# A third seven-product block in chunk 0's feed-forward: four plain tiles regrouped, and the channel sums of w_out's first pieces moved ahead

## The chip, the cores and the metric

The kernel runs on one core of a Trainium2 chip. The metric is the device time of one execution in microseconds, as the median of several runs. A core has five engines with queues of their own: TensorE (PE in the profile; its weight loads are shown apart as PEld), VectorE (DVE), ScalarE (ACT), GpSimd (POOL) and SyncE (SP, which here only issues DMAs). Each engine works through its own queue in order; engines wait for each other through semaphores.

## What is computed

The reference is polysketch attention followed by an MLP with exact GELU:

```python
# q, k, v: (4, 4, 1088, 32) float32;  S1, S2: (8, 32)
def phi(x):
    a = np.einsum('rd,bhsd->bhsr', S1, x)
    b = np.einsum('rd,bhsd->bhsr', S2, x)
    return np.einsum('bhsi,bhsj->bhsij', a, b).reshape(*x.shape[:-1], 64)
q_p, k_p = phi(q), phi(k)
kv  = np.einsum('bhsf,bhsd->bhfd', k_p, v)
z   = np.sum(k_p, axis=2)
num = np.einsum('bhsf,bhfd->bhsd', q_p, kv)
den = np.einsum('bhsf,bhf->bhs', q_p, z)[..., None] + 1e-06
x   = (num / den).transpose(0, 2, 1, 3).reshape(4352, 128)
h   = x @ w_in                                  # w_in:  (128, 2048)
out = (0.5 * h * (1 + erf(h / sqrt(2)))) @ w_out  # w_out: (2048, 128)
```

The weights and the sketch matrices arrive as 64-bit floats; the kernel rounds them to 32 bits itself.

## The kernel before

**Tiling.** Tokens are worked on in nine chunks: eight of 512 tokens (two per batch entry, chunk 0 to 7) and a last one (chunk 8) with the 64 tokens that are left of each batch entry. d_ff is cut into 16 tiles of 128, numbered fi = 0 to 15. For each chunk n and tile fi, `hidden` (L740) multiplies a tile of w_in with the chunk's xT into a PSUM bank `h_ps` (two banks in rotation), and ACT applies GELU from there into SBUF (L747). The output of a chunk is accumulated in PSUM banks `o_ps` (two in rotation).

**Two ways to multiply with w_out.** A *plain* tile is one 128x512 matmul (`project`, L925) from a buffer `g` (four in rotation) into one bank. A *block* takes four tiles together. Each pair of tiles is a 2x2 problem, two halves of the tokens and two halves of the output channels, and is done with seven products of half size instead of eight (`two_products`, L826). The products are 64 output rows wide and 256 columns long; two run side by side on the two halves of TensorE, so a block is seven pairs. They need *token sums* (four combinations of GELU outputs, made on POOL in `token_sums`, L791 to L794, in buffers called bits_low, bits_a, bits_e, bits_m, in this order) and *channel sums* (four combinations of w_out, T1 to T4 in the buffers called small, made on POOL in `channel_sums`, L778 to L781, once for each of five pieces of w_out). The products are numbered: "4" and "7" use the first token sum (7) and T4 and T3, "6" uses bits_e, "1" and "5" use bits_a, "2" and "3" use bits_m. A block that opens a chunk's banks has the order 4/7 (two pairs), 6 (one), 1/5 (two), 2/3 (two). At the end of a chunk `drain` and `combine` put the products together, and the plain tiles' sum, copied out of its bank earlier by `take_usual` (L854, ACT), is added.

Before the change, chunks 0 and 1 have eight plain tiles each (`USUAL = 8`), then two blocks; chunks 2 to 7 have four blocks; chunk 8 has six pairs of another form.

**Pieces of the weights.** w_in and w_out are loaded in five pieces, columns 0 to 256, 256 to 512, 512 to 1024, 1024 to 1536, 1536 to 2048 (piece 0 to 4). Each is rounded by a chain of instructions in class `Rounding`: the low words scaled (`low_words`, L270, ACT), the exponent and mantissa fields (`fields`, L283 and L288, DVE), the exponents (`exponents`, L294, ACT), the mantissas (`mantissas`, L302, DVE), the signs (`signs`, L307, DVE) and the product (L312, DVE, or POOL for the last pieces). The token sums of the blocks use the same rotating buffers as this rounding, and the GELU outputs of a block use the big buffers in which the raw weights of pieces 2 to 4 landed.

**Order.** The order of each engine's queue is the order of the text; nothing is scheduled. `steps` lists (chunk, tile) one after the other: step t does `hidden` for its tile, then (if the tile ends a block) the token sums, then what has been hung on `slots[t]` with `at(t, ...)`, then `products[t]`. Before, the steps were chunk 0 tiles 0 to 3, chunk 1 tiles 0 to 3, chunk 0 tiles 4 to 7, chunk 1 tiles 4 to 7 (steps 0 to 15), chunk 0 tiles 8 to 15, chunk 1 tiles 8 to 15 (steps 16 to 31), then chunks 2 to 8. A plain product stands two steps after its tile (`LAG`). From step 18 on a hidden tile is two 64-row halves side by side. Slots used by the change and its neighbourhood: rounding of pieces 2 and 3 of both weights (slots 4 to 11), of w_in's piece 4 (12 and 13) and of w_out's piece 4 (14 and 15); `spread_sketches` on POOL (11); `widen_v_rem`, the v remainder, on POOL (12); the key transposes `key_turn_blocks` on DVE (14, L383); `features_of_all`, which multiplies the transposed keys with the sketches on PE (16, L1043); `outer_of_all` and `add_tokens` on DVE (16, 17), whose result `z_sum` and `kv_sum` on PE want at step 24 (L456).

Of the kernel before, what the change touches and what calls it, by code (L numbers as in the profile page):

```python
# [10 lines left out]
AX = mybir.AluOpType  # L11
# [5 lines left out]
def kernel(  # L17
# [18 lines left out]
    pe, dve, act, pool, sp = nc.tensor, nc.vector, nc.scalar, nc.gpsimd, nc.sync  # L36
# [5 lines left out]
    NF = d_ff // 128  # L42
# [7 lines left out]
    NCH = J // JC  # L50
    C = D + 1
    LAG = 2
    NMAIN = B * NCH
    NB = 4

    USUAL = 8
    BLOCKED = 12
    NCHUNK = NMAIN + 1
    assert B == 4 and d_model == 128 == H * D == JC * D == 2 * F and H == 4 and REM == 64 and NCH == 2
# [18 lines left out]
    def hidden_bank():  # L78
        return hps.tile([128, CW], FP, name="h_ps")

    def out_bank():
        return ops.tile([128, CW], FP, name="o_ps")


    by_act, by_dve, by_pool = act.copy, dve.tensor_copy, pool.tensor_copy
# [11 lines left out]
    w_in_sb = [big.tile([d_model, c1 - c0], FP, name=f"w_in{i}") for i, (c0, c1) in enumerate(pieces)]  # L97
    w_out_sb = [big.tile([128, c1 - c0], FP, name=f"w_out{i}") for i, (c0, c1) in enumerate(pieces)]
# [42 lines left out]
    def block(dtype=U32):  # L141

        b = big.tile([128, NB, 512], U32, name="block", bufs=3)
        return b if dtype == U32 else b.bitcast(dtype)
# [108 lines left out]
    class Rounding:  # L253
# [11 lines left out]
                self.low = self.lows[:rows, n:2 * n] if beside else self.lows[:rows, :n]  # L265
                self.m = mlp.tile([128, LC], FP, name="bits_m")[:rows, :n]

        def low_words(self):
            if self.wide:
                act.activation(out=self.low, in_=self.lo, func=ACT.Copy, scale=2.0 ** -52)  # L270

        def fields(self, by_dve=False):
# [454 lines left out]
    def w_tile(w, fi):  # L727
        i = max(i for i, (c0, c1) in enumerate(pieces) if c0 <= fi * 128)
        at = fi * 128 - CUTS[i]
        return w[i][:, at:at + 128]  # L730
# [3 lines left out]
    def hidden(n, fi, by_halves=False):  # L734
        W = width[n]
        ps = first_banks.pop((n, fi)) if (n, fi) in first_banks else hidden_bank()
        w = w_tile(w_in_sb, fi)
        for rows in (slice(0, 64), slice(64, 128)) if by_halves else (slice(0, 128),):
            if (n, fi) not in begun:
                pe.matmul(ps[rows, :W], lhsT=w[:, rows], rhs=xT[n][:, :W], start=True, stop=True)  # L740
        if n < NCH and fi < USUAL:
            g_of[n, fi] = mlp.tile([128, CW], FP, name="g", bufs=4)
        else:
            if fi % NB == 0:
                blocks[n, fi // NB] = block(FP)
            g_of[n, fi] = blocks[n, fi // NB][:, fi % NB]
        act.activation(out=g_of[n, fi][:, :W], in_=ps[:, :W], func=ACT.Gelu)  # L747
# [60 lines left out]
        return sums[n, b][j][:, e], T[j][:, k]  # L808

    def first_block(n):  # L810
        return USUAL // NB if n < NCH else 0

    def two_products(n, b, i):

        fours, ones_, sixes = [("4", "7", e, e) for e in range(2)], [("1", "5", e, e) for e in range(2)], ("6a", "6b", 0, 1)

        opens = b == first_block(n)
        order = fours + ([sixes] + ones_ if opens else ones_ + [sixes]) + [("2", "3", e, e) for e in range(2)]
        two = order[i]
        if opens and i == 0:  # L820
            acc[n] = [out_bank(), out_bank()]
        for name, e in zip(two[:2], two[2:]):
            half, bank, col = PLACE[name]
            moving, fixed = factor(n, b, name, e)

            pe.matmul(acc[n][bank][half * 64:(half + 1) * 64, col:col + HW], lhsT=fixed, rhs=moving,  # L826
                      start=opens and e == 0 and name in "4715", stop=b == NF // NB - 1, skip_group_check=True)
# [24 lines left out]
    def take_usual(n):  # L852
        usual[n] = mlp.tile([128, CW], FP, name="g", bufs=4)
        act.copy(out=usual[n], in_=o_of[n])  # L854
# [14 lines left out]
    def sums_rem(k):  # L869
        g = [g_of[NMAIN, 2 * k + i][:, :256].rearrange("p (half x) -> p half x", half=2) for i in range(2)]  # L870
        (a11, a21), (a12, a22) = ([a[:, h] for h in range(2)] for a in g)
        s = mlp.tile([128, CW], FP, name="g", bufs=4).rearrange("p (j x) -> p j x", j=4)
        eng = dve if k > 3 else pool
        eng.tensor_sub(out=s[:, 2], in0=a11, in1=a21)
        eng.tensor_add(out=s[:, 0], in0=a21, in1=a22)
        eng.tensor_sub(out=s[:, 1], in0=s[:, 0], in1=a11)
        eng.tensor_sub(out=s[:, 3], in0=a12, in1=s[:, 1])
        sums[NMAIN, k] = s
# [33 lines left out]
        drained[NMAIN] = to  # L912

    def project(n, fi, parts=range(B // 2), cols=slice(None)):
        first, final = fi == (BLOCKED if n == NMAIN else 0), fi == (USUAL if n < NCH else NF) - 1
        if first and n not in o_of:
            o_of[n] = out_bank() if n < NMAIN else [out_bank() for i in range(B // 2)]
        g = g_of[n, fi]
        if n == NMAIN:

            for i in parts:
                pe.matmul(o_of[n][i][:, :128], lhsT=g[:, i * 128:(i + 1) * 128], rhs=w_tile(w_out_sb, fi),  # L922
                          start=first, stop=final)
            return
        pe.matmul(o_of[n][:, cols], lhsT=w_tile(w_out_sb, fi), rhs=g[:, cols], start=first, stop=final)  # L925
# [35 lines left out]
    r = Rounding(SR)  # L961
# [64 lines left out]
        first_hidden(0, half)  # L1026


    steps = [(n, fi) for f in range(0, USUAL, 4) for n in range(NCH) for fi in range(f, f + 4)]
    steps += [(n, fi) for n in range(NCHUNK) for fi in range(USUAL if n < NCH else 0, NF)]  # L1030
    slots = {t: [] for t in range(len(steps) + LAG)}

    def at(t, f, *a):
        slots[t].append(lambda: f(*a))
# [85 lines left out]
            attend(n, banks)  # L1120
        take_kv(b, banks[:, 1, CW // 2:])

    def round_at(t, w, product_by=dve):
        r = []
        at(t, lambda: (r.append(Rounding(w)), r[0].low_words(), r[0].fields()))
        at(t + 1, lambda: (r[0].exponents(), r[0].mantissas(), r[0].signs(), r[0].product(product_by)))

    for i, (t0, t1) in enumerate(((4, 6), (8, 10))):
        round_at(t0, w_in_sb[i + 2])
        round_at(t1, w_out_sb[i + 2])  # L1130
    round_at(12, w_in_sb[4], pool)
    at(13, channel_sums, 3)

    at(12, widen_v_rem, 1)
    for r in range(2):
        at(14, key_turn_blocks, 1, r)
    round_at(14, w_out_sb[4], pool)
    at(15, query_turn, 2)
    at(16, features_of_all, 1)
    at(16, outer_of_all, 1)  # L1140
# [9 lines left out]
    at(24, query_sketch, 2)  # L1150
    at(26, lambda: turn_kv(1, held["kv"]))
    at(24, query_outer, 2)
    for i, t in enumerate((25, 26, 28)):
        at(t, channel_sums, i)
    at(11, spread_sketches)
    at(40, repeat_first_z)
    for n in range(3, NCHUNK):

        t = (n - 1) * NF
# [39 lines left out]
    products = {t: [] for t in range(len(steps) + LAG)}  # L1199
    done = {t: [] for t in range(len(steps) + LAG + 1)}  # L1200
    drains = {t: [] for t in range(len(steps) + LAG + 1)}
    for t, (n, fi) in enumerate(steps):
        if n < NCH and fi < USUAL:
            products[t + LAG].append((project, n, fi))
            if fi == USUAL - 1:
                slots[t + LAG + 1 + 2 * n].append(lambda n=n: take_usual(n))
        elif n == NMAIN:
            if fi % 2 and fi < BLOCKED:
                slots[t].append(lambda k=fi // 2: sums_rem(k))
            at_ = t + LAG  # L1210
            if fi == NF - 1:

                names = [(k, name) for k in range(BLOCKED // 2) for name in ORDER_REM]
                steps_rem = NF - 5
                for i, (k, name) in enumerate(names):
                    products[n * NF + 5 + i * steps_rem // len(names)].append((product_rem, k, name))
                products[n * NF + 4 + steps_rem].append((combine_rem,))

                products[at_] += [(project, n, NF - f, (i,)) for f, i in ((4, 0), (3, 0), (2, 0), (4, 1), (1, 0), (3, 1),
                                                                          (2, 1), (1, 1))]  # L1220
                done[at_ + 1].append(n)
        elif fi % NB == NB - 1:
            b = fi // NB
            opens = b == first_block(n)
            late = int(n < NCH or n == NCH and opens)
            for later, pairs in ((3, 3), (4, 2), (5, 2)) if opens else ((2, 2), (3, 2), (4, 1), (5, 2)):
                later += late
                for i in range(pairs):
                    products[t + later].append((two_products, n, b, len([p for q in products.values() for p in q
                                                                        if p[:3] == (two_products, n, b)])))  # L1230
            if b == NF // NB - 1:
                drains[t + 6 + late].append(n)
                done[t + (12 if n < NMAIN - 1 else 9)].append(n)

    for t in range(len(steps) + LAG):
# [40 lines left out]
        if t < len(steps):  # L1276
            n, fi = steps[t]
            hidden(n, fi, by_halves=t >= 18)
        if t < len(steps) and steps[t][0] < NMAIN and steps[t][1] % NB == NB - 1:
            n, b = steps[t][0], steps[t][1] // NB  # L1280
            if b >= first_block(n):
                token_sums(n, b)
# [48 lines left out]
```

## Time and profile before

| what | us |
|---|---|
| median of 3 runs (lowest, highest) | 258.04 (258.0, 258.37) |
| the profiled execution's own time | 257.91 |
| its span, first to last instruction | 256.1 |
| PE busy | 251.9 |
| POOL busy | 171.7 |
| DVE busy | 156.0 |
| ACT busy | 114.5 |
| hidden tiles (L740) on PE | 137.1 |
| plain products (L925) on PE | 16.5 |

The granted TensorE clock was 1.000 over the span. The page's table by engine counts the time in which an engine has an instruction under way; for PE the ends of matmuls are modelled, so the distance between the starts of two rows says more than a row's length. In a timeline row the columns are the start, the length, the engine, the line, the operation, output <- inputs with shape, and the number of instructions merged; behind it in brackets stands how long the engine was idle before and what ended that. A float32 matmul shows as two records.

### The profile page before, as it was taken

The page shows a single profiled execution, that of the slowest core. Times are in us where ns is not written, and L with a number is a line of the kernel's source. Part 1 is how long each engine was busy: PE and PEld are TensorE (multiplying, and loading weights), DVE is VectorE, ACT ScalarE, POOL GpSimd, SP SyncE. Part 2 cuts the span into 40 slices and gives each one's busy share as a digit, 9 for nine tenths or more (in the row PEclk, how much of TensorE's full clock was granted, in tenths as well). Part 3 has the DMA queues.
Part 4 walks back from the last instruction along what each step waited for, and adds up shares of the span by engine and source line. Part 5 has one row for each costly group of instructions (what it writes and reads, how often), then busy time and mean ns, then how long its engine had stood idle before and what let it go on. Part 6 is the DMA issues. An engine that isn't in the chain of part 4 may idle for free.

```text
span 256.1 us, 5952 instructions
## 1 busy us (share of the span) xinstructions
PE 251.9 (98%) x2407; PEld 131.5 (51%) x2407; DVE 156.0 (61%) x330; ACT 114.5 (45%) x221; POOL 171.7 (67%) x191
## 2 busy tenths in 40 slices
PE   8999999999999999999999999999999999999994
PEld 4755444255454545454444455455544444445784
DVE  4896889969698987580278976399307000700382
ACT  3784766523535333533335332623444334433541
POOL 3413008799969777587758774787758777877950
PEclk9999999999999999999999999999999999999999
DMA  6789548610001101101000001000200200020021
GB/s 209 217 280 292 153 122 205 204 26 12 0 3 17 25 4 23 21 13 31 0 3 0 0 15 31 1 4 0 38 6 7 37 0 4 5 36 3 0 36 31
DMA packets 29083, 13.50 MB, mean 53 GB/s; under 512 B 21888, under 2 KB 27264, under 8 KB 29056
## 3 DMA queue, kind: packets, MB, share of 16 engines
q1 hardware_dynamic: 28624, 12.79, 20.1%
q8 instruction: 19, 0.31, 0.5%
q10 hardware_dynamic: 432, 0.33, 0.4%
q14 instruction: 8, 0.07, 0.1%
HBM read 10.88 MB, written 2.23 MB: 51 GB/s over the span
## 4 chain that ended last, share of the span: by engine, by line
PE 98%; ACT 0%; DVE 0%; issue 0%
PE h_ps L740 45%; PE o_ps L826 33%; PE o_ps L925 5%; PE w_ps L896 2%; PE w_ps L456 1%; PE w_ps L604 1%; PE w_ps L659 1%; PE w_ps L957 1%; PE w_ps L570 1%; PE o_ps L922 1%; PE h_ps L756 1%; PE o_ps L445 1%; PE w_ps L1043 1%; PE h_ps L348 1%; PE w_ps L685 0%; PE o_ps L397 0%
## 5 line engine op out<-in xcount | busy, mean ns | idle before, releaser
L740 PE MATMUL h_ps<-xT,w_in 128*64 128x512 f32 (+2 forms) x536 | 137.1, 568 | 0.0
L747 ACT ACTIVATE block<-h_ps 128x512 f32<-128x512 f32 (+1 forms) x128 | 73.0, 571 | 116.3 <-PE h_ps L740 114.4
L826 PE MATMUL o_ps<-block,w_out 128*64 128x256 f32 x224 | 57.5, 379 | 0.0
L740 PEld LDWEIGHTS h_ps<-xT,w_in 128*64 128x64 f32 (+1 forms) x536 | 40.7, 140 | 30.3 <-issue 11.6
L791 POOL TENSOR_TENSOR bits_low<-block 128x512 f32<-128x512 f32 x28 | 36.3, 1296 | 27.4 <-ACT block L747 27.4
L826 PEld LDWEIGHTS o_ps<-block,w_out 128*64 128x64 f32 x224 | 30.5, 137 | 38.0 <-issue 27.5
L792 POOL TENSOR_TENSOR bits_a<-block 128x512 f32<-128x512 f32 x28 | 35.7, 1276 | 11.7 <-ACT block L747 11.6
L841 DVE COPY sums<-o_ps 64x256 f32<-64x256 f32 x8 | 3.3, 417 | 60.6 <-PE o_ps L826 60.6
L793 POOL TENSOR_TENSOR bits_e<-bits_a,block 128x512 f32<-128x512 f32 x28 | 36.0, 1287 | 2.2
L794 POOL TENSOR_TENSOR bits_m<-block,bits_e 128x512 f32<-128x512 f32 x28 | 35.8, 1277 | 2.2
L826 PE MATMUL o_ps<-block,small 128*64 128x256 f32 x112 | 28.8, 379 | 0.0
L826 PE MATMUL o_ps<-bits_low,small 128*64 128x256 f32 x112 | 28.8, 379 | 0.0
L826 PE MATMUL o_ps<-bits_a,small 128*64 128x256 f32 x112 | 28.8, 379 | 0.0
L826 PE MATMUL o_ps<-bits_m,w_out 128*64 128x256 f32 x112 | 28.7, 379 | 0.0
L826 PEld LDWEIGHTS o_ps<-block,small 128*64 128x64 f32 x112 | 15.2, 137 | 17.9 <-issue 10.8
L826 PE MATMUL o_ps<-bits_e,small 128*64 128x256 f32 x112 | 17.1, 383 | 0.0
L925 PE MATMUL o_ps<-g,w_out 128*128 128x512 f32 (+1 forms) x34 | 16.5, 572 | 0.0
L826 PEld LDWEIGHTS o_ps<-bits_m,w_out 128*64 128x64 f32 x112 | 15.3, 137 | 0.0
L616 DVE STREAM_TRANSPOSE w_ps<-w_ps 128x512 f32<-128x512 f32 (+1 forms) x7 | 4.8, 687 | 17.1 <-ACT xT L670 12.7
L826 PEld LDWEIGHTS o_ps<-bits_a,small 128*64 128x64 f32 x112 | 15.2, 137 | 0.0
L826 PEld LDWEIGHTS o_ps<-bits_low,small 128*64 128x64 f32 x112 | 15.2, 137 | 0.0
L826 PEld LDWEIGHTS o_ps<-bits_e,small 128*64 128x64 f32 x112 | 7.7, 137 | 10.6 <-issue 8.8
(223 smaller groups left out, 318.5 us busy)
## 6 DMA issues: line engine op xcount, KB each, us to landing
block<-in_moe_w_in_dram SPq DMA_DIRECT2D x3, 512.0 KB, 9.8
block<-in_moe_w_out_dram SPq DMA_DIRECT2D x3, 512.0 KB, 12.0
k<-in_k_dram SPq DMA_DIRECT2D x12, 128.0 KB, 2.7
v<-in_v_dram SPq DMA_DIRECT2D x12, 128.0 KB, 3.6
q<-in_q_dram SPq DMA_DIRECT2D x24, 64.0 KB, 2.4
out_dram<-oT SPq DMA_DIRECT2D x21, 64.0 KB, 2.2
q_first<-in_q_dram SPq DMA_DIRECT2D x2, 256.0 KB, 3.8
v<-in_v_dram SPq DMA_DIRECT2D x2, 256.0 KB, 4.1
```

The source lines that it names most:

```text
L348: pe.transpose(ps[:, i * 128:(i + 1) * 128], in_=s, identity=ident)
L616: dve.transpose(out=tok, in_=ps[:, :, :H2])
L740: pe.matmul(ps[rows, :W], lhsT=w[:, rows], rhs=xT[n][:, :W], start=True, stop=True)
L747: act.activation(out=g_of[n, fi][:, :W], in_=ps[:, :W], func=ACT.Gelu)
L791: pool.tensor_sub(out=s[3], in0=a11, in1=a21)
L792: pool.tensor_add(out=s[1], in0=a21, in1=a22)
L793: pool.tensor_sub(out=s[2], in0=s[1], in1=a11)
L794: pool.tensor_sub(out=s[4], in0=a12, in1=s[2])
L826: pe.matmul(acc[n][bank][half * 64:(half + 1) * 64, col:col + HW], lhsT=fixed, rhs=moving, start=opens and e == 0 and name in "4715", stop ...
L841: dve.tensor_copy(out=N[lo, 0, one], in_=a0[lo, one])
L896: pe.matmul(acc[NMAIN][rows, COLS_REM[name]], lhsT=tokens[:, rows], rhs=fixed, start=k == 0 and name == ORDER_REM[0], stop=k == BLOCKED // ...
L925: pe.matmul(o_of[n][:, cols], lhsT=w_tile(w_out_sb, fi), rhs=g[:, cols], start=first, stop=final)
```

## The change

Chunk 0 keeps four plain tiles (0 to 3); its tiles 4 to 7 become a block like the others, the third of its chunk. All eight plain tiles of chunk 1 now stand ahead of chunk 0's tiles 4 to 15: steps 0 to 3 are chunk 0's plain tiles, 4 to 11 chunk 1's, 12 to 23 chunk 0's tiles 4 to 15, 24 to 31 chunk 1's tiles 8 to 15. The plain products of tiles 5, 6 and 7 are put off by one, two and two steps, so that those of chunk 1 fall on steps 6 to 10, 12, 14 and 15, and steps 11, 13, 16 and 17 have none. Chunk 0's new block has its token sums at step 15 and its seven pairs at steps 19, 20 and 21 (two, three, two); the second block of chunk 0 then has its products at steps 22 to 25 in the order of a block that doesn't open.

The rounding of the last pieces: the low words of w_in's and w_out's piece 4 are made by POOL, in slots 10 and 12, instead of ACT in slots 12 and 14. The channel sums of pieces 0, 1 and 2 move from slots 25, 26 and 28 to 5, 6 and 8, those of piece 3 from 13 to 12. In slot 14 the fields of w_out's piece 4 now stand ahead of the key transposes in DVE's queue. The plain sums are copied out of their banks in slots 12 and 17, not 14 and 20.

```diff
-    USUAL = 8
+    USUAL = [4, 8]
...
-        def low_words(self):
-            if self.wide:
+        def low_words(self, by_pool=False):
+            if self.wide and by_pool:
+                pool.tensor_scalar(out=self.low, in0=self.lo, scalar1=2.0 ** -52, scalar2=None, op0=AX.mult)
+            elif self.wide:
                 act.activation(out=self.low, in_=self.lo, func=ACT.Copy, scale=2.0 ** -52)
...
-        if n < NCH and fi < USUAL:
+        if n < NCH and fi < USUAL[n]:
...
-        return USUAL // NB if n < NCH else 0
+        return USUAL[n] // NB if n < NCH else 0
...
-    steps = [(n, fi) for f in range(0, USUAL, 4) for n in range(NCH) for fi in range(f, f + 4)]
-    steps += [(n, fi) for n in range(NCHUNK) for fi in range(USUAL if n < NCH else 0, NF)]
+    steps = [(n, fi) for n in range(NCH) for fi in range(USUAL[n])]
+    steps += [(n, fi) for n in range(NCHUNK) for fi in range(USUAL[n] if n < NCH else 0, NF)]
...
-    def round_at(t, w, product_by=dve):
+    def round_at(t, w, product_by=dve, low=None):
         r = []
-        at(t, lambda: (r.append(Rounding(w)), r[0].low_words(), r[0].fields()))
+        at(t if low is None else low, lambda: (r.append(Rounding(w)), r[0].low_words(by_pool=low is not None)))
+        at(t, lambda: r[0].fields())
         at(t + 1, lambda: (r[0].exponents(), r[0].mantissas(), r[0].signs(), r[0].product(product_by)))
...
-    round_at(12, w_in_sb[4], pool)
-    at(13, channel_sums, 3)
+    round_at(12, w_in_sb[4], pool, low=10)
+    round_at(14, w_out_sb[4], pool, low=12)
+    at(12, channel_sums, 3)
...
-    round_at(14, w_out_sb[4], pool)
...
-    for i, t in enumerate((25, 26, 28)):
+    for i, t in enumerate((5, 6, 8)):
         at(t, channel_sums, i)
...
-            products[t + LAG].append((project, n, fi))
-            if fi == USUAL - 1:
-                slots[t + LAG + 1 + 2 * n].append(lambda n=n: take_usual(n))
+            products[t + LAG + (0, 0, 0, 0, 0, 1, 2, 2)[fi]].append((project, n, fi))
+            if fi == USUAL[n] - 1:
+                slots[(12, 17)[n]].append(lambda n=n: take_usual(n))
...
-            for later, pairs in ((3, 3), (4, 2), (5, 2)) if opens else ((2, 2), (3, 2), (4, 1), (5, 2)):
+            for later, pairs in ((3, 2), (4, 3), (5, 2)) if opens and n == 0 else ((3, 3), (4, 2), (5, 2)) if opens else ((2, 2), (3, 2), (4, 1), (5, 2)):
```

The lines in the prediction are those of the kernel before; in the changed one those behind the first hunk stand two or three further down.

More of the change, by code (lines that the diff above doesn't have):

```diff
@@ L914, in project @@
     def project(n, fi, parts=range(B // 2), cols=slice(None)):
-        first, final = fi == (BLOCKED if n == NMAIN else 0), fi == (USUAL if n < NCH else NF) - 1
+        first, final = fi == (BLOCKED if n == NMAIN else 0), fi == (USUAL[n] if n < NCH else NF) - 1
         if first and n not in o_of:
@@ L1202 @@
     for t, (n, fi) in enumerate(steps):
-        if n < NCH and fi < USUAL:
-            products[t + LAG].append((project, n, fi))
-            if fi == USUAL - 1:
-                slots[t + LAG + 1 + 2 * n].append(lambda n=n: take_usual(n))
+        if n < NCH and fi < USUAL[n]:
+            products[t + LAG + (0, 0, 0, 0, 0, 1, 2, 2)[fi]].append((project, n, fi))
+            if fi == USUAL[n] - 1:
+                slots[(12, 17)[n]].append(lambda n=n: take_usual(n))
         elif n == NMAIN:
```

## The prediction

> **What bounds the kernel now.** The page first: the engine table and the chain of waits.
>
> ```profile
> PE 251.9 (98%) x2407; PEld 131.5 (51%) x2407; DVE 156.0 (61%) x330; ACT 114.5 (45%) x221; POOL 171.7 (67%) x191
> PE 98%; ACT 0%; DVE 0%; issue 0%
> ```
>
> TensorE is busy from end to end and the chain is TensorE alone, so time can be won in two ways: fewer matmul columns, or less waiting inside the runs that count as busy. Every other engine matters only where it makes TensorE wait. So I read the timeline of the touched stretch, 20 to 60 us, one engine at a time.
>
> ```profile
> 41.64 1.02 PE L740 MATMUL h_ps<-xT,w_in 128*128 128x512 f32 x2
> 42.59 0.66 PE L1043 MATMUL w_ps<-kT,S_ab 64*32 64x256 f32 x16
> ...
> 46.25 5.69 PE L740 MATMUL h_ps<-xT,w_in 128*64 128x512 f32 x24
> 51.77 0.38 PE L826 MATMUL o_ps<-block,small 128*64 128x256 f32 x1
> ```
>
> What counts is the distance from start to start. The first row is step 16's hidden tile. The third is six hidden tiles in a row (steps 18 to 23) with no product between them.
>
> ```profile
> 36.08 0.69 DVE L312 TENSOR_TENSOR w_out<-bits_m,bits_e 128x512 f32<-128x512 f32 x1
> 36.69 0.42 DVE L283 TENSOR_SCALAR bits_e<-block 128x512 uint32<-128x512 uint32 x1
> ...
> 38.79 0.69 DVE L307 SCALAR_TENSOR_TENSOR bits_e<-block,bits_r 128x512 uint32<-128x512 uint32 x1 [0.54 <-ACT bits_r L294]
> 39.40 1.30 DVE L383 STREAM_TRANSPOSE kT<-k 128x512 f32<-128x512 f32 x2
> 40.62 0.54 DVE L283 TENSOR_SCALAR bits_e<-block 128x512 uint32<-128x512 uint32 x1
> 41.07 0.68 DVE L288 TENSOR_SCALAR bits_a<-block 128x512 uint32<-128x512 uint32 x1
> 41.86 0.76 DVE L302 SCALAR_TENSOR_TENSOR bits_m<-bits_a,bits_low 128x512 f32<-128x512 uint32 x1
> 42.54 0.94 DVE L307 SCALAR_TENSOR_TENSOR bits_e<-block,bits_r 128x512 uint32<-128x512 uint32 x1
> 43.41 0.70 DVE L554 STREAM_TRANSPOSE qT<-q 128x512 f32<-128x512 f32 x1
> ```
>
> ```profile
> 39.56 1.31 POOL L312 TENSOR_TENSOR w_in<-bits_m,bits_e 128x512 f32<-128x512 f32 x1 [3.37 <-DVE bits_e L307]
> 40.82 0.65 POOL L778 TENSOR_TENSOR small<-w_out 128x128 f32<-128x128 f32 x1
> ...
> 43.01 0.78 POOL L781 TENSOR_TENSOR small<-w_out,small 128x128 f32<-128x128 f32 x1
> 43.76 1.29 POOL L312 TENSOR_TENSOR w_out<-bits_m,bits_e 128x512 f32<-128x512 f32 x1
> 45.13 0.46 POOL L778 TENSOR_TENSOR small<-w_out 128x128 f32<-128x128 f32 x1
> ...
> 48.05 1.28 POOL L791 TENSOR_TENSOR bits_low<-block 128x512 f32<-128x512 f32 x1 [1.10 <-ACT block L747]
> ...
> 53.24 1.27 POOL L791 TENSOR_TENSOR bits_low<-block 128x512 f32<-128x512 f32 x1
> ```
>
> POOL's first token sums start at 48.05, after both products of the last weight pieces and the channel sums of pieces 3 and 4. Read 40.6 to 43.8 on both engines together: piece 3's channel sums take 2.94 us (40.82 to 43.76) where piece 4's take 1.82 (45.13 to 46.95), and the four rounding instructions beside them run 0.54, 0.68, 0.76 and 0.94 instead of 0.42, 0.42, 0.69 and 0.69. VectorE and POOL slow each other there.
>
> **The matmuls that go.** Plain hidden tiles and products alternate from step 5 (22.76) to step 15 (39.93): 20 of them in 17.17 us, 0.858 each. Four plain products go: 3.43. A block is seven pairs of 64-row products; two pairs take 0.86 (57.69 to 58.55), so 3.02 comes. Won: 0.41.
>
> **The wait that goes.** Six hidden tiles cost 6 x 0.858 = 5.15; from 46.25 to 51.77 they took 5.52. With 0.05 for the first half after a change of tile width (46.25 to 46.73 instead of 0.43), 0.32 is left as waiting for the two hidden banks that ACT empties. In the changed order only steps 18 and 19 stand together, so I count all of it as won. Sum so far: -0.73.
>
> **TensorE's new dates, nothing late.** Two products fewer stand before step 16: its tile starts at 39.93, and the key sketches (L1043), which need the two key transposes of slot 14, could start at 39.93 + 0.86 + 0.09 = 40.88. From there to step 22's first block products (the second block's "4" and "7", which need its first token sum): sketches 0.59, transpose 0.17, tile 0.86, remainder keys 0.17, change of width 0.15, tiles 0.91 and 0.86, then two pairs 0.86, tile 0.86, three pairs 1.30, tile 0.86, two pairs 0.86, tile 0.86. That is 9.31, so 50.19.
>
> **VectorE's transposes.** They now stand behind the two field instructions of the last w_out piece. Before, they ended at 40.70. Now piece 3's channel sums start as soon as its product is written (36.77 at best), beside the same four rounding instructions as at 40.62. By those rows e to the fifth instruction is 2.79 (40.62 to 43.41), so the fields start near 36.9 + 2.79 = 39.7, the transposes near 40.5 and end near 41.8: TensorE would wait 0.9 at L1043. With no slowing (e to a 0.33, a to mantissas 0.52, then 0.62, 0.61, 0.33 and 0.45) they end at 40.84: no wait. Bounds 0 to 1.0.
>
> **POOL's queue, the longest chain.** What is queued, in order: channel sums of pieces 0 and 1, piece 2 (waits for its product, 29.91), low words of w_in's last piece, the sketch spreading (1.79 in its rows), low words of w_out's last, piece 3's channel sums, the v remainder, w_in's product, the new block's four token sums, w_out's product, piece 4's channel sums, and only then the second block's token sums. Piece 2's sums meet the same rounding instructions: 29.93 + 2.94 = 32.87. Low words on POOL are in no row. Bounds: a one-input copy and a two-input sum of the same 512 columns.
>
> ```profile
> L360 POOL COPY sums<-v 128x512 f32<-128x512 f32 x1 | 0.6, 612 | 1.7 <-DMA v<-in_v_dram 1.7
> L791 POOL TENSOR_TENSOR bits_low<-block 128x512 f32<-128x512 f32 x28 | 36.3, 1296 | 27.4 <-ACT block L747 27.4
> ```
>
> With one tensor read it is nearer the copy; since VectorE's two-input work runs beside it I take 0.9: POOL is through at 32.87 + 0.9 + 1.79 + 0.9 = 36.46. Piece 3's sums need VectorE's product, which ends at 36.77 undisturbed; its signs and the product now run beside POOL work, up to 0.25 longer each (0.94 against 0.69). I take 37.05. Then 2.94, v remainder 0.5 (memset 0.20, copy 0.30): w_in's product starts at 40.49. Behind it 1.26 (39.56 to 40.82), four token sums 5.19 (48.05 to 53.24), w_out's product 1.37, piece 4's sums 1.82, the second block's first sum 1.28, and 0.05 to TensorE: 51.46. TensorE is ready at 50.19 plus its earlier wait (0.9), so the two waits end together at 51.46: 1.27 late against the undisturbed order, the wait for the transposes included. Bounds: with piece 3's sums undisturbed (1.82) and 36.82 as start, w_in's product starts at 39.14 and the sum lands at 50.11, no wait; with low words of 1.28, piece 3 starts at 37.3, meets more two-input work and the sum lands near 52.2, 2.0 late.
>
> The Trainium skill, SBUF — State Buffer, section "Who interferes with whom", states that VectorE's second port pair is shared with GpSimd and held as a lock for a whole instruction: a VectorE instruction with two SBUF inputs, or in a two-port mode, and a reading GpSimd instruction block each other outright. By that rule the sum would come out as in rival 3's second half; the rows above agree with the direction, not with the full size, and I go by their 2.94.
>
> **What costs nothing, and its cover.** ACT loses two low-word passes (0.68 each); its chain is not TensorE's, so nothing is won. Channel sums of pieces 0 and 1 (eight of 0.32) move to about 19.8 to 22.5, beside the last half of xT, which ends at 21.58 and is needed at 22.33, and w_out's piece 1, ready at 21.02 and needed at 21.47: 0.45 covers two instructions lengthened by at most 0.25 (0.05 lost at worst). Copying chunk 1's plain sum out (0.58, slot 17) ends some 3.0 after the sketches start, 0.7 before its bank is wanted. The key features behind the late transposes reach their end near 52.6 plus some slowing, TensorE wants them near 55.0. POOL's relief behind step 24 buys nothing: the products there wait for no token sum. DMA issues and their order on SP stay as they were.
>
> **The sum.** -0.41 - 0.32 + 1.27 = +0.54. On the profiled execution's own time, 257.91 (span 256.1), that is 258.45; it lies 0.13 under the median 258.04, so the median becomes 258.6.
>
> **The rivals.** (1) *The saving arrives, faster.* POOL's shifted sums and the rounding hardly meet, w_in's product starts by 39.2 and both waits vanish: -0.73 with up to 0.1 of waiting, 257.35. For it: POOL idles 3.37 before that product today and VectorE waits 0.54 for ACT at every second rounding step, so there is slack; against it, the same eight instructions meeting at 40.8. It decides where w_in's product starts before 39.7. (2) *Only the transposes wait.* POOL's sums are partly undisturbed and land before TensorE, but the sketches wait 0.7 to 0.97: -0.73 + 0.83 = +0.1, 258.1. It needs w_in's product by 40.1. (3) *A dearer POOL.* The low words cost 1.28 or more and push all behind: -0.73 + 2.0, 259.3. Or the eight instructions that meet are strung out one behind the other: 1.82 + 2.08 (the undisturbed steps 0.33, 0.52, 0.62 and 0.61 of the rounding) = 3.90 instead of 2.94, so 0.96 on top of the forecast: 259.55. For it: the low words' input is integer and every second word; against it, the 0.61 copy, and the 2.94 that the rows show for the very same eight. (The second half is what the SBUF page's rule, full blocking, would make of it.)
>
> **Chances.** Forecast (+0.2 to +0.9) 0.50; rival 1 0.16; rival 2 0.22; rival 3 0.12. About 0.2% (0.5 us) is what a measurement of this kernel can tell. Of the forecast some 0.34 lies above that and 0.16 within; rival 2 lies within, rival 3 above. So faster 0.16, same 0.38, slower 0.46. Likeliest case alone: 258.2 to 258.95. Range for 8 in 10, from rival 1 to rival 3: 257.3 to 259.4.
>
> **What would show it.** Right: a gap on TensorE ahead of L1043's successor up to 0.9, waiting for VectorE's kT; a second ahead of the second block's first products, waiting for POOL's token sum; piece 3's channel sums near 2.9 us in all; TensorE's later rows shifted by one constant from step 24 on. Wrong: w_in's product on POOL before 39.7, TensorE without gaps between 40 and 52, or a new wait before 23 us or after 60.

## The result, and the profile after

The changed kernel takes 262.02 us, the median of 6 runs (261.92 to 262.44), against 258.03 (257.99 to 258.5) of the kernel before, run beside it: 1.0153 times as long, 95% interval 1.014 to 1.0166. Slower was the likelier side of the forecast; the size, +3.99 against +0.54, lies far outside the range (257.3 to 259.4).

The profiled execution took 262.44, with a span of 260.7. From the page of the changed kernel, the row of the engines and the row of the chain of waits:

```profile
PE 254.2 (98%) x2427; PEld 133.9 (51%) x2427; DVE 159.4 (61%) x330; ACT 113.4 (44%) x219; POOL 183.8 (71%) x197
PE 88%; POOL 9%; issue 1%; DVE 1%; ACT 0%; POOLq 0%
```

Before, the chain was TensorE alone. Now 9% of it, some 23 us, runs through POOL. TensorE's busy share is still 98%, and its busy time rose by 2.3 us although its matmul columns became fewer: of the 4.5 us of waiting found below, only 2.5 show as idle time of PE (0.96 and 1.54, in brackets in the rows), so the rest is counted as busy. So again the distance from start to start counts.

The timeline of the changed kernel, TensorE (start, duration, instruction):

```profile
40.73 1.02 PE L742 MATMUL h_ps<-xT,w_in 128*128 128x512 f32 x2
41.68 1.13 PE L1045 MATMUL w_ps<-kT,S_ab 64*32 64x256 f32 x16
42.74 0.33 PE L350 MATMUL w_ps<-ident,k_rem 128*128 128x128 f32 x1
...
45.79 0.59 PE L828 MATMUL o_ps<-block,small 128*64 128x256 f32 x2
...
49.20 0.65 PE L828 MATMUL o_ps<-bits_e,small 128*64 128x256 f32 x4 [0.96 <-POOL bits_e L795]
...
53.13 0.59 PE L828 MATMUL o_ps<-block,small 128*64 128x256 f32 x2
55.26 0.43 PE L828 MATMUL o_ps<-bits_low,small 128*64 128x256 f32 x1 [1.54 <-POOL bits_low L793]
...
56.61 0.59 PE L828 MATMUL o_ps<-block,w_out 128*64 128x256 f32 x2
57.03 0.38 PE L828 MATMUL o_ps<-bits_a,small 128*64 128x256 f32 x1
...
57.90 1.02 PE L742 MATMUL h_ps<-xT,w_in 128*64 128x512 f32 x3
58.92 0.32 PE L458 MATMUL w_ps<-k_s,ones 128*32 128x64 f32 x8
```

Five waits can be read off. The key sketches (41.68 to 42.74) take 1.06 instead of the 0.59 of before: the second transpose is late, 0.47. From the new block's first pairs to its next (45.79 to 49.20), two pairs and a hidden tile worth 1.72 take 3.41: 1.69. The same distance for the second block (53.13 to 56.61) is 3.48: 1.76. The next one, worth 1.82 in a run without waits (e5 below), is 2.31 (56.61 to 58.92): 0.49. The matmuls of L458 themselves lose another 0.08. Together 4.49.

The table of waits of the changed kernel from 40 to 61 us, the engine's weight loads (total us, times, longest):

```profile
PEld o_ps L828 <- POOL bits_low L793: 2.4, 2, 2.0
...
PEld o_ps L828 <- POOL bits_e L795: 1.8, 1, 1.8
PEld w_ps L458 <- DVE k_s L1075: 0.9, 1, 0.9
...
PEld o_ps L828 <- POOL bits_a L794: 0.3, 1, 0.3
```

So TensorE waits for POOL's token sums in both blocks. The wait for VectorE's k_s looks larger than it is: of the 0.49, 0.42 is lost ahead of it, where the half of TensorE that multiplies bits_a runs that much behind the other (57.03 against 56.61). The table names POOL's second token sum there; no run separates it from the lag that the wait for the first sum left. From the tile's last rows to L458 it is 1.02 (57.90 to 58.92), and 0.95 in e3 below, where k_s is ready 6 us earlier: 0.07 for k_s. That makes 3.87 for POOL's sums, 0.47 for the transposes and 0.15 for k_s. What made POOL late is in its own timeline, of the changed kernel:

```profile
33.82 2.05 POOL L270 TENSOR_SCALAR bits_low<-block 128x512 f32<-128x512 uint32 x1
35.94 0.30 POOL L498 TENSOR_TENSOR own_r<-mask 128x2 f32<-128x2 f32 x1
...
38.00 1.24 POOL L508 COPY S_abc<-S_abc 128x64 f32<-128x64 f32 x3
39.33 2.04 POOL L270 TENSOR_SCALAR bits_low<-block 128x512 f32<-128x512 uint32 x1
41.45 0.46 POOL L780 TENSOR_TENSOR small<-w_out 128x128 f32<-128x128 f32 x1
...
43.20 0.20 POOL L366 MEMSET v_rem_aug<- 128x128 f32 x1
...
43.72 1.30 POOL L314 TENSOR_TENSOR w_in<-bits_m,bits_e 128x512 f32<-128x512 f32 x1
44.98 1.27 POOL L793 TENSOR_TENSOR bits_low<-block 128x512 f32<-128x512 f32 x1
...
47.55 1.60 POOL L795 TENSOR_TENSOR bits_e<-bits_a,block 128x512 f32<-128x512 f32 x1
49.23 1.61 POOL L796 TENSOR_TENSOR bits_m<-block,bits_e 128x512 f32<-128x512 f32 x1
50.80 1.30 POOL L314 TENSOR_TENSOR w_out<-bits_m,bits_e 128x512 f32<-128x512 f32 x1
...
53.94 1.27 POOL L793 TENSOR_TENSOR bits_low<-block 128x512 f32<-128x512 f32 x1
```

No instruction of POOL waits for another engine from 33.82 to 53.94. The low words (L270) take 2.05 each, 2.12 from start to start. The spreading of the sketches (35.94 to 39.33) takes 3.39 instead of 1.79: queued behind piece 2's channel sums, it now runs beside VectorE's rounding. Piece 3's channel sums (41.45 to 43.20) take an undisturbed 1.75, because they come after that rounding and no longer beside it.

VectorE, the same stretch of the changed kernel:

```profile
34.20 0.86 DVE L285 TENSOR_SCALAR bits_e<-block 128x512 uint32<-128x512 uint32 x1
34.99 0.41 DVE L290 TENSOR_SCALAR bits_a<-block 128x512 uint32<-128x512 uint32 x1
...
40.83 1.29 DVE L385 STREAM_TRANSPOSE kT<-k 128x512 f32<-128x512 f32 x2
45.05 2.98 DVE L304 SCALAR_TENSOR_TENSOR bits_m<-bits_a,bits_low 128x512 f32<-128x512 uint32 x1 [2.94 <-POOL w_in L314]
47.95 1.75 DVE L309 SCALAR_TENSOR_TENSOR bits_e<-block,bits_r 128x512 uint32<-128x512 uint32 x1
...
58.45 0.42 DVE L1075 TENSOR_TENSOR k_s<-w_ps,k_p_rem 64x256 f32<-64x256 f32 x1
```

The mantissas of w_out's last piece (L304) wait 2.94 for POOL's product of w_in's last piece. They don't read it: bits_m has two buffers, and their tile can only have got the one in which w_in's mantissas lie, so they may write once the product has read it (with a third buffer, in e3, the wait is gone). Then they and the signs meet POOL's back-to-back token sums and take 2.98 and 1.75 instead of 0.69 each, and two of the token sums 1.60 instead of 1.27. All that VectorE has queued behind (the key features, up to k_s) is late too.

One part of the difference lies ahead of the changed stretch. The rows of before and after are the same up to the first hidden tiles, and these start at 13.77 before and at 14.57 after, 0.80 later, ahead of anything that was changed; in the runs below the same row lies 0.08 to 0.80 later. Why is open. So I compare a stretch that begins behind it and holds all that comes out different on TensorE: from step 16's hidden tile (40.73 after; 41.64 before, less the two plain products of 0.86 that stood ahead of it there, 39.93) to the hidden tile behind chunk 1's first "4" and "7" (65.03 and 60.49). It is 20.57 before and 24.31 after: +3.74. With the 0.80 that is the whole difference of the two profiled executions (262.44 and 257.91, 4.53).

| kernel | median us | ratio to before (95%) | stretch us | waits in it |
|---|---|---|---|---|
| before | 258.03 to 258.55 | 1 | 20.57 | |
| after | 262.02 | 1.0153 (1.014 to 1.0166) | 24.31 | 4.5 |
| e1_act_low | 259.67 | 1.0053 (1.0038 to 1.0068) | 21.98 | 2.2 |
| e2_spread_early | 260.48 | 1.0085 (1.007 to 1.01) | 22.58 | 2.8 |
| e3_third_m_buffer | 262.21 | 1.0149 (1.0132 to 1.0166) | 24.22 | 4.4 |
| e4_all_four | 258.73 | 1.001 (0.9998 to 1.0022) | 20.71 | 0.9 |
| e5_fields_early | 257.59 | 0.9968 (0.9959 to 0.9978) | 19.78 | 0 |
| e6_turns_first | 258.55 | 1.0002 (0.9993 to 1.0012) | 20.69 | 0.9 |

The waits are each stretch less that of e5, in which TensorE waits for no other engine. The kernel before had a median of 258.47 beside e1 to e4 and 258.55 beside e5 to e8, up to 0.5 above the 258.03 beside the changed kernel, so a run is compared with the changed kernel by its ratio or its stretch and not by its median.

### The profile page after: what moved, and what is told of

It reads as the page before. It is cut to its first block, busy times and chain, and to the rows that moved or that the text cites. A ratio compares the mean times of both kernels' runs of the same rounds, so it can differ in the third digit from the quotient of the medians.

```text
span 260.7 us, 5999 instructions
## 1 busy us (share of the span) xinstructions
PE 254.2 (98%) x2427; PEld 133.9 (51%) x2427; DVE 159.4 (61%) x330; ACT 113.4 (44%) x219; POOL 183.8 (71%) x197
## 4 chain that ended last, share of the span: by engine, by line
PE 88%; POOL 9%; issue 1%; DVE 1%; ACT 0%; POOLq 0%
PE h_ps L742 39%; PE o_ps L828 33%; PE w_ps L898 2%; PE o_ps L927 2%; POOL bits_low L270 2%; PE w_ps L458 2%; PE w_ps L606 1%; PE w_ps L661 1%; PE w_ps L959 1%; PE w_ps L572 1%; POOL bits_low L793 1%; PE o_ps L924 1%; PE h_ps L758 1%; PE h_ps L350 1%; POOL small L783 1%
## 5 line engine op out<-in xcount | busy, mean ns | idle before, releaser
L742 PE MATMUL h_ps<-xT,w_in 128*64 128x512 f32 (+2 forms) x536 | 138.5, 568 | 0.0
L749 ACT ACTIVATE block<-h_ps 128x512 f32<-128x512 f32 (+1 forms) x132 | 75.4, 571 | 122.2 <-PE h_ps L742 117.0
L828 PE MATMUL o_ps<-block,w_out 128*64 128x256 f32 x232 | 59.5, 379 | 0.0
L793 POOL TENSOR_TENSOR bits_low<-block 128x512 f32<-128x512 f32 x29 | 37.4, 1288 | 28.3 <-ACT block L749 28.3
L828 PEld LDWEIGHTS o_ps<-block,w_out 128*64 128x64 f32 x232 | 31.7, 137 | 38.5 <-issue 27.7
L794 POOL TENSOR_TENSOR bits_a<-block 128x512 f32<-128x512 f32 x29 | 37.0, 1277 | 12.4 <-ACT block L749 12.2
L795 POOL TENSOR_TENSOR bits_e<-bits_a,block 128x512 f32<-128x512 f32 x29 | 37.7, 1299 | 2.3
L796 POOL TENSOR_TENSOR bits_m<-block,bits_e 128x512 f32<-128x512 f32 x29 | 37.6, 1295 | 2.3
L828 PE MATMUL o_ps<-block,small 128*64 128x256 f32 x116 | 30.2, 380 | 0.0
L927 PE MATMUL o_ps<-g,w_out 128*128 128x512 f32 (+1 forms) x26 | 12.4, 564 | 0.0
```

The source lines that it names most:

```text
L793: pool.tensor_sub(out=s[3], in0=a11, in1=a21)
L794: pool.tensor_add(out=s[1], in0=a21, in1=a22)
L795: pool.tensor_sub(out=s[2], in0=s[1], in1=a11)
L796: pool.tensor_sub(out=s[4], in0=a12, in1=s[2])
```

## The experiments

Two readings of these rows were open. A: POOL's queue, lengthened by the low words and by the slowed spreading, sets the end. B: the shared buffer does it, by bringing the mantissas onto the token sums. The first three runs each change one thing.

**e1_act_low: the last pieces' low words by ACT again, in the new slots.**

```diff
-        at(t if low is None else low, lambda: (r.append(Rounding(w)), r[0].low_words(by_pool=low is not None)))
+        at(t if low is None else low, lambda: (r.append(Rounding(w)), r[0].low_words()))
```

> The changed kernel, but the low words of the last two pieces are made by ACT again (same slots 10 and 12). Theory A (POOL's queue ahead of the token sums is too long; two low-word passes of 2.05 us stand in it): POOL loses 4.2 us, but piece 3's channel sums can't start before VectorE's product (about 37.6 with this execution's start), so w_in's product comes some 2.6 us earlier than 43.7 and TensorE's waits between 41 and 60 us fall from 4.5 to about 1.9: 259.4. Theory B (the w_out mantissas share a bits_m buffer with w_in's product, wait for it and then run against the token sums): the wait stays, so over 261. If both low words were hidden anyway: 262.

259.67, 1.2 above the kernel before beside it instead of 3.99; the stretch is 2.33 shorter than the changed kernel's (21.98 against 24.31), with one instruction for each of two pieces moved off POOL. The timeline of e1, POOL:

```profile
36.98 0.57 POOL L780 TENSOR_TENSOR small<-w_out 128x128 f32<-128x128 f32 x1 [0.71 <-DVE w_out L314]
...
39.81 0.49 POOL L366 MEMSET v_rem_aug<- 128x128 f32 x1
...
40.69 1.28 POOL L314 TENSOR_TENSOR w_in<-bits_m,bits_e 128x512 f32<-128x512 f32 x1
41.94 1.26 POOL L793 TENSOR_TENSOR bits_low<-block 128x512 f32<-128x512 f32 x1
...
47.77 1.29 POOL L314 TENSOR_TENSOR w_out<-bits_m,bits_e 128x512 f32<-128x512 f32 x1
```

Without the low words POOL is back at the dates of the prediction: piece 3's channel sums start at 36.98 (37.05 in the prediction) and take 2.83 (2.94), w_in's product starts at 40.69 (40.49). B alone is out: the buffer is still shared here, but the product comes 3.03 earlier (0.68 of it the earlier start of this execution), so the mantissas wait only 0.22 for it. They still take 2.98 beside the token sums, and these 5.83 (41.94 to 47.77).

**e2_spread_early: the sketches spread in slot 4, ahead of all this.**

```diff
-    at(11, spread_sketches)
+    at(4, spread_sketches)
```

> The changed kernel, but the sketch spreading stands in slot 4, ahead of the channel sums of pieces 0 to 2, where POOL is idle (it is 3.4 us of the busy stretch now). Theory A: POOL's queue is shorter by up to 3.4, w_in's product some 2.2 us earlier, 259.8. Theory B: over 261. If it is contention alone that sets POOL's pace, the instructions behind it slow down in its place and less than 1 us is won.

260.48; the stretch is 1.73 shorter than the changed kernel's (22.58 against 24.31), where about 2.2 was expected. The spreading takes 1.78 there, as before, and is a second part of POOL's lateness, but it isn't added to the first: in e1 it takes 3.25 as well (33.02 to 36.27) and hides behind the wait for piece 3's product, 0.71 of which is left. The miss is in the transposes: POOL being early, piece 3's channel sums now meet the rounding again, the transposes start at 41.41, and TensorE's sketches lose 1.43 there in place of 0.47.

**e3_third_m_buffer: a third buffer for bits_m** (and one instead of two for two small tiles, to make room).

```diff
-                self.m = mlp.tile([128, LC], FP, name="bits_m")[:rows, :n]
+                self.m = mlp.tile([128, LC], FP, name="bits_m", bufs=3)[:rows, :n]
```

> The changed kernel with three bits_m buffers instead of two (room for it from bits_high and z_cols with one buffer each), so that the mantissas of w_out's last piece no longer wait for w_in's product on POOL. Theory A: POOL's queue stays as long; only the token sums' slowing (0.6) and TensorE's wait for k_s (0.4) can go: 261.0 to 262. Theory B: 260 or less.

262.21, 3.74 above the kernel before beside it; the stretch is 0.09 shorter: next to nothing. The timeline of e3, POOL, then VectorE, then TensorE:

```profile
42.27 0.91 POOL L782 TENSOR_TENSOR small<-w_out,small 128x128 f32<-128x128 f32 x1
...
44.49 1.30 POOL L314 TENSOR_TENSOR w_in<-bits_m,bits_e 128x512 f32<-128x512 f32 x1
```

```profile
42.04 0.82 DVE L304 SCALAR_TENSOR_TENSOR bits_m<-bits_a,bits_low 128x512 f32<-128x512 uint32 x1
...
52.49 0.42 DVE L1075 TENSOR_TENSOR k_s<-w_ps,k_p_rem 64x256 f32<-64x256 f32 x1
```

```profile
58.01 1.02 PE L742 MATMUL h_ps<-xT,w_in 128*64 128x512 f32 x3
58.96 0.32 PE L458 MATMUL w_ps<-k_s,ones 128*32 128x64 f32 x8
```

The wait of 2.94 is gone, the mantissas come at 42.04 instead of 45.05, k_s is ready at 52.9 instead of 58.87, and the token sums keep their 1.27. But the mantissas now meet piece 3's channel sums, and w_in's product starts 0.77 later (44.49 against 43.72). The second block's wait shrinks from 1.76 to 1.42 and k_s's 0.15 goes, but the first block's grows from 1.69 to 2.15. The 0.42 ahead of L458 stays, though k_s has long been ready. By itself the shared buffer cost next to nothing; its wait stood beside a longer one.

**e4_all_four: the three edits, with piece 3's channel sums in slot 16 and piece 4's in slot 20.**

```diff
-    at(12, channel_sums, 3)
+    at(16, channel_sums, 3)
...
-    at(18, channel_sums, 4)
+    at(20, channel_sums, 4)
```

> The changed kernel with low words by ACT, spreading in slot 4, three bits_m buffers, and the channel sums of pieces 3 and 4 each put behind the token sums that stand next (slots 16 and 20). Theory A: w_in's product starts as soon as VectorE's signs are written (about 39.5 with a start like the changed kernel's), the second block's first token sum lands before TensorE wants it, and of the waits only up to 0.3 for the key transposes is left: 258.03 - 0.73 + 0.2 = 257.5 (257.3 to 257.9). If the wait that I book as won (0.32) or the pairs (0.41) are not won: 258 or more.

A miss: 258.73, level with the kernel before (258.47 beside it), where 0.5 less was expected. No wait for POOL is left, but one that the expectation did not have. The timeline of e4, VectorE and then POOL and TensorE:

```profile
38.78 0.42 DVE L285 TENSOR_SCALAR bits_e<-block 128x512 uint32<-128x512 uint32 x1
39.11 1.53 DVE L290 TENSOR_SCALAR bits_a<-block 128x512 uint32<-128x512 uint32 x1
40.56 1.29 DVE L385 STREAM_TRANSPOSE kT<-k 128x512 f32<-128x512 f32 x2
```

```profile
38.94 1.42 POOL L314 TENSOR_TENSOR w_in<-bits_m,bits_e 128x512 f32<-128x512 f32 x1 [2.67 <-DVE bits_e L309]
```

```profile
41.41 1.14 PE L1045 MATMUL w_ps<-kT,S_ab 64*32 64x256 f32 x16 [0.39 <-DVE kT L385]
```

POOL being free, w_in's product starts as soon as VectorE has written the signs, so it meets the two fields that the change put ahead of the transposes: the second takes 1.53 instead of 0.42 and ends 0.3 after the product. The transposes end 1.1 later, and TensorE's sketches lose 0.93 (41.41 instead of 40.95 at their start, and 1.07 instead of 0.59 for themselves).

**e5_fields_early: e4, and w_out's last piece taken apart:** its fields in slot 10, ahead of w_in's rounding; mantissas and signs behind the transposes; its product on POOL in slot 20, behind the second block's token sums. (`round_at` itself is extended so that it takes these slots.)

```diff
-    round_at(14, w_out_sb[4], pool, low=12)
+    round_at(14, w_out_sb[4], pool, low=12, begin=10, fields=10, last=20)
```

> As e4, and the last port meetings taken out of the way: the fields of w_out's last piece in slot 10 (ahead of any POOL work beside them), so that the key transposes follow the signs of w_in's last piece at once, and w_out's product on POOL behind the second block's token sums (slot 20). Theory C (a field instruction of 0.42 that meets w_in's product on POOL waits until that ends: 1.53 in e4, and the transposes and TensorE with it): the wait of 0.93 at the key sketches goes, no wait on POOL comes in its place, and the whole 0.73 is won: 0.6 to 0.8 less than the kernel before. If the transposes' wait is not due to that meeting, the time stays at that of e4 (0.3 above the kernel before).

257.59 in 10 runs, 0.9968 of the kernel before (0.9959 to 0.9978): faster than both kernels. The page of e5, and its timeline of VectorE and of TensorE:

```profile
PE 98%; ACT 0%; DVE 0%; issue 0%
```

```profile
38.88 1.30 DVE L385 STREAM_TRANSPOSE kT<-k 128x512 f32<-128x512 f32 x2
40.09 0.79 DVE L304 SCALAR_TENSOR_TENSOR bits_m<-bits_a,bits_low 128x512 f32<-128x512 uint32 x1
40.81 1.76 DVE L309 SCALAR_TENSOR_TENSOR bits_e<-block,bits_r 128x512 uint32<-128x512 uint32 x1
```

```profile
40.04 1.02 PE L742 MATMUL h_ps<-xT,w_in 128*128 128x512 f32 x2
40.99 0.66 PE L1045 MATMUL w_ps<-kT,S_ab 64*32 64x256 f32 x16
41.59 0.33 PE L350 MATMUL w_ps<-ident,k_rem 128*128 128x128 f32 x1
```

The chain is TensorE alone again. Mantissas and signs still meet a product and a token sum on POOL (1.76 for the signs), but nothing that ends last stands behind either. The stretch is 0.79 shorter than before: what the new order of the tiles is worth when nothing waits.

**e6_turns_first: e4 with the key transposes ahead of w_out's fields,** as they stood before.

```diff
+    for r in range(2):
+        at(14, key_turn_blocks, 1, r)
     round_at(12, w_in_sb[4], pool, low=10)
     round_at(14, w_out_sb[4], pool, low=12)
...
-    for r in range(2):
-        at(14, key_turn_blocks, 1, r)
```

> As e4, but the key transposes stand ahead of the fields of w_out's last piece, as in the kernel before. Theory C: no wait at the key sketches, but the fields, mantissas and signs now all meet POOL's product and token sums and each waits for one POOL instruction; the key features end some 1 us later than in e4, and TensorE waits for k_s at step 24 by 0.5 to 1.7: from 0.2 less to 1.0 more than the kernel before. If the four pass between POOL's instructions without delay: 0.7 less.

258.55, level with before. The wait at the sketches is gone, as expected, and 0.91 of waiting is back further down: all four rounding instructions now meet POOL's product and token sums (0.53, 1.50, 1.64 and 1.76), the second block's first sum comes 0.19 late, the half that multiplies bits_a lags by 0.42 as in the changed kernel, and k_s comes 0.22 late with 0.08 behind it. Turning two VectorE instructions around against two others only changes who is late.

**e7_low_words_contiguous and e8_low_words_as_float: why 2.05?** The low words are every second word of an integer tensor. e7 reads 512 adjacent integer words in their place, e8 every second word as float. Both leave out the right low words of these two pieces. The edit of e7, then that of e8:

```diff
-                pool.tensor_scalar(out=self.low, in0=self.lo, scalar1=2.0 ** -52, scalar2=None, op0=AX.mult)
+                pool.tensor_scalar(out=self.low, in0=raw[self.dst.name].rearrange("p n two -> p (n two)")[:, :512], scalar1=2.0 ** -52, scalar2=None, op0=AX.mult)
```

```diff
-                pool.tensor_scalar(out=self.low, in0=self.lo, scalar1=2.0 ** -52, scalar2=None, op0=AX.mult)
+                pool.tensor_scalar(out=self.low, in0=self.hi.bitcast(FP), scalar1=2.0 ** -52, scalar2=None, op0=AX.mult)
```

> Measures one price, in the changed kernel: POOL's low-word instruction reads 512 words that lie side by side instead of every second word (so the low words of the last two pieces are not the right ones). If the stride sets the 2.05 us, it falls to 0.6 to 1.0 (one-input copy of 512 columns: 0.61); if the integer input or the operation sets it, it stays near 2.05.

> Measures the same price with the input read as float, every second word as before (the high words are taken, so the low words of the last two pieces are not the right ones). If the conversion from integer sets the 2.05 us, it falls to 1.3 or less; if it is the operation or the stride, it stays.

The instruction groups of line 270, of e7 and then of e8 (shortest, median and longest, ns):

```profile
L270 POOL TENSOR_SCALAR bits_low<-block x2: 2008/2010/2012, 33.3 to 38.8; 128x512 f32<-128x512 uint32 x2
```

```profile
L270 POOL TENSOR_SCALAR bits_low<-block x2: 2037/2050/2062, 33.8 to 39.3; 128x512 f32<-128x512 f32 x2
```

2.01 and 2.05 against 2.04: neither the stride nor the conversion makes the price by itself (0.03 at most). What within POOL does is open. The two were not taken away together, and VectorE worked beside the instruction each time that it ran (the shortest took 1.95, in e2). A multiplication by a constant in another form, such as a product of two tensors (1.30 in the rows of L314), was not tried. The times of these single runs, 261.91 and 262.43, are close to those of the changed kernel.

## Why the prediction failed

**The step that failed** is the price of POOL's low words: "with one tensor read it is nearer the copy; since VectorE's two-input work runs beside it I take 0.9", between 0.61 and 1.28. They take 2.05, outside of both bounds. The bounds were of the same columns and the same engine but of other operations, and nothing in the trace tied them to this one; a row of the operation itself was missing, and the bound "two tensors cost more than one" was an assumption. Rival 3 had the right mechanism in its first half (a dearer POOL, 259.3) and was held down to a chance of 0.12 by the same bounds.

**How it grew.** w_in's product was forecast at 40.49 and started at 43.72, or 42.92 without the later start of the whole execution: 2.43 late. By rows: low words, 2 x (2.12 - 0.9) = +2.44; spreading, 3.39 instead of 1.79, +1.60; piece 3's channel sums, 1.75 instead of 2.94, -1.19; the forecast's 0.59 of idling ahead of them, gone; three smaller ones +0.17. The spreading is a second term of the same kind: I took 1.79 from its rows of before, where it ran from 19.79 on, and put it into a stretch in which VectorE rounds 512-column pieces nearly without a break. Alone it would have stayed hidden, as e1 shows; behind low words of 2.12 it counts in full. Either correction by itself leaves some of the loss (2.2 of waits in e1, 2.8 in e2).

**Token sums, 5.19.** They took 5.82, because mantissas and signs fell onto them. I had read VectorE's late work only for the transposes, not for what came behind. In e1 this is +0.64 on the same chain.

**"The key features ... reach their end near 52.6 plus some slowing, TensorE wants them near 55.0."** The cover was gone: k_s was ready at 58.87. The mantissas' wait for the shared buffer, which I had not seen, and 4.6 us for two instructions ate the 2.4. It cost little, 0.07 at L458 and 0.08 behind it, since TensorE was late by then too.

**The first block.** I had its token sums land in time, and let the two blocks' lateness fall due at once in the second. With POOL 2.4 later it was due in the first: 1.69, then 1.76 in the second and another 0.42 behind its first pairs, which the sum had no term for.

**The transposes, 0.9.** 0.47 in after, with piece 3's channel sums out of their way; but 0.81 in e1 and 0.93 in e4, where POOL is as early as the forecast had it. The mechanism stands; in e4 it was another POOL instruction than I had named.

**What was right.** -0.41 for the plain products and -0.32 for the two hidden banks: -0.73 forecast, -0.79 in the stretch of e5. Piece 3's channel sums at 2.94 where they meet the rounding (2.83 in e1; 1.75 where they don't). The channel sums of pieces 0 to 2 moved up, ACT's passes and the plain sums' copies cost nothing: up to step 16 the rows of after run at the distances of before (26.16 from the first hidden tile to step 16's tile, in both). And it was POOL's queue that decided, as forecast.

The sum by the stretch: -0.79 in a stretch without waits, +4.53 of waits, 3.74; the rest of the 3.99 is within how much the start varies.

## What to carry to other kernels

Before an instruction is moved to another engine, find a row of that operation on that engine; where there is none, the rows of other operations need not bound it (here they did not), and it is worth running one such instruction by itself. A duration also belongs to its neighbours: an instruction that is moved beside another engine's work has to be priced there, and so has everything queued behind it. A change that wins little on the engine that bounds the kernel should leave the others' order alone until their slack in that very stretch is counted: here the same new tile order was worth -0.8 with the queues rearranged, and +4 as it was made.

## What the hardware showed

**POOL's multiplication by a constant is dear.** 512 columns cost 2.05 us (4.0 ns a column), and 2.01 and 2.05 with the stride or the integer type of the input taken away, one at a time, where POOL's sum of two tensors of that size takes 1.27 and its copy 0.61. The Trainium skill, GPSIMD Engine Reference, section "Engine selection", states that one-input work on GpSimd runs at roughly line rate and only two-input work about half as fast as on VectorE. The rows here say otherwise: this one-input form is the slowest of the three.

**Where VectorE meets a two-input sum or product of 512 columns on POOL, it loses about what is left of that instruction.** e4's field started 0.17 after POOL's product and took 1.53 instead of 0.42; the mantissas in after began with a token sum of 1.27 and ended 0.55 after a second one; the third token sum, which started 0.48 before they ended, took 0.33 more. The Trainium skill, SBUF — State Buffer, section "Who interferes with whom", states an exclusive lock for a whole instruction, in which the loser blocks altogether. For instructions of 1.3 us the trace agrees. For piece 3's short channel sums of 0.45 it agrees only in part: strung out one behind the other they and the rounding would take 3.90, and they took 2.83 in e1. Beside the low words it doesn't hold: the field at 34.20, behind a low-word instruction that runs from 33.82 to 35.87, took 0.86 instead of 0.42, and the next one (34.99) ran within that instruction in its usual 0.41. Transposes (one input) ran at 1.29 beside POOL's product in e1, as if alone, which agrees with the same section: a VectorE instruction with one input outside the two-port modes does not contend. The fields read one tensor too and were delayed; no trace here shows what sets them apart.
